# An S4 convolution with an MLP on one core: filter taps by products of two channels, a residual and some joins on TensorE, and a new order of the work

## The chip, the core and the metric

The kernel runs on one core of a Trainium2 chip. A core has five engines with their own instruction streams: TensorE (PE, matrix products; its weight loads are listed apart as PEld), VectorE (DVE), ScalarE (ACT), GpSimd (POOL) and SyncE (SP, which here issues nearly all DMAs). They meet only through semaphores. The metric is the device time of one execution in microseconds (us); a smaller one is better.

## The reference

One sequence of L = 2048 rows and D = 512 channels goes through a diagonal state space convolution and an MLP, each with a residual:

```
def _A_ref(u, A_re, A_im, B_re, B_im, C_re, C_im, log_dt, Dskip):
    logdA = dt * A                                   # dt = exp(log_dt), A complex, D x N, N = 128
    P = jnp.exp(logdA[:, :, None] * l[None, None, :])
    K = jnp.einsum("dn,dnl,dn->dl", Cc, P, dB).real  # the filter: 2048 taps for each channel
    Kf, Uf = rfft2(pad(K)), rfft2(pad(u.T))
    return irfft2(Uf * Kf)[..., :L].T + u * Dskip
def _B_ref(x, w1, b1, w2, b2):
    h = gelu(layernorm(x) @ w1 + b1)                 # 512 -> 1376
    return h @ w2 + b2                               # 1376 -> 512
x = A_u
h = x + _A_ref(layernorm(x), ...)
h2 = h + _B_ref(layernorm(h), ...)
```

## The kernel before

**Tiling.** The 2048 rows are two blocks (b = 0 and 1) of 1024; the 512 channels are four chunks (c = 0 to 3) of 128, and two chunks make a pair (q = 0: chunks 0 and 1; q = 1: chunks 2 and 3). The convolution of 2048 taps becomes three products of spectra: block 0 by the filter's first half, block 1 by the first half, and block 0 by the second half into block 1. Tiles on TensorE are up to 128 x 1024 float32 in PSUM, of which there are four slots; each matrix product is followed by an evacuation (`evac`), a cast to bfloat16 in SBUF that ScalarE (L542) or VectorE (L544) does.

**Stages, by line.**
- `chain` (L1030, L1059, L1068, L1072) and `aexps` (L801) make, for each channel and state, the powers that the taps are built from: sines on ScalarE, products on VectorE, angles on TensorE.
- Taps: `kgen` (L1101 and L1102) for chunks 0 and 1, one channel for each matmul, weights of 20 columns in four column strips of the array. `kgen4` (L1132 and L1133) for chunks 2 and 3: weights of 128 columns hold four channels, the right side too (4 x 33 columns), so the product has all 16 pairs of channels of which the four of a channel with itself are used; the evacuation takes the whole tile, and the tap store `Kg[1]` has room for it. L1115 and L1142 add the skip term to the first tap.
- `carry` (L1152, four small copies for each pair, on SyncE's queue), then `kspec` (L1167) makes the filter's first spectrum step; `kstage` writes it to DRAM (`AK_d`) and reads it back in another layout by the DMA helper L554; `fstage` (L981) finishes it. `lstage` (L1195, L1214, by way of `AL_d`) does the same for the taps of the second half.
- `xspec` (L961, L981) makes the spectra of the rows.
- `inverse` for each block and chunk, in two halves fh: products of spectra on VectorE (L1243; one for block 0, two for block 1, added by L1248). For block 1 two further VectorE operations (L1251) join real and imaginary parts before TensorE; 16 matmuls L1259 follow. For block 0 there is no join, and TensorE does 32 matmuls that add the parts in PSUM. After the evacuation a transposing DMA (`turn`, L1265) gives the layout for the tail.
- `tail(b, sb)`, for halves sb of a block: L1329 spreads the result back over the rows, and the residual x is added: in block 0's first half by TensorE (an identity product, L1324, evacuated as a cast), in the other three by VectorE (L1336). L1339 takes statistics; `stats` holds the small operations and a power on GpSimd (L926); L1352 or L1354 normalises.
- `mlp(b, sb)`: L1383, gelu on ScalarE (L1385), L1405, the last addition on VectorE (L1407), stores.

**What sets the order.** Each operation is recorded with `add(engine, cost, ...)` in the order of the code. The list `ORDER` then says in which order they are issued: its n-th entry is the number of an operation (as ~i, a negative number, where an operation that two engines could do goes to the second one). Each engine executes its own operations in that order, and SyncE issues its DMAs in that order. Costs that a recorded operation names move nothing in `ORDER`; `Sched.run` uses them to estimate where TensorE would wait for more than 0.4 us behind a certain point, and puts filler matmuls there (L1510, results unused).

Of the kernel before, what the change touches and what calls it, by code (L numbers as in the profile page):

```python
# [15 lines left out]
P = 128  # L16
# [10 lines left out]
NB = 33  # L27
# [138 lines left out]
class VS(V):  # L166
# [244 lines left out]
def kernel(ctx, tc, A_u, A_A_re, A_A_im, A_B_re, A_B_im, A_C_re, A_C_im, A_log_dt, A_Dskip,  # L411
# [85 lines left out]
    S4 = take(f16, 4, 512)  # L497
    assert pos[0] <= rest0 + 8192
    pos[0] = rest0 + 8192
    Kg = [take(bf16, NB, 2, 32), at(sc0 - 512, bf16, NB, 4, 2, 32)]  # L500
    zlo = take(bf16, NB, 2, 32).lo
    AK0 = take(bf16, 16, 2 * CW).lo
    XB = XT(ar, (E0 + 16384, BA0 + 16384))
# [613 lines left out]
    def kgen4(c, pr):  # L1117
        Ar, Br, Ai, Bi = EA2[c - 2], EB[c], IA2[c - 2], IB[c]
        kg = Kg[1]
        for j0 in range(0, 32, 6):  # L1120
            S.pr = pr + 0.01 * (j0 // 6)
            p = Ps()
            n = min(6, 32 - j0)
# [20 lines left out]
    def kgof(q, g):  # L1144
        return Kg[0].ap() if q == 0 else Kg[1].ap()[:, :, g]
# [406 lines left out]
```

## Time and profile before

| | before |
|---|---|
| time, median of 3 runs | 235.97 us (235.88 to 236.08) |
| the profiled execution, its own time | 235.89 us |
| its span in the trace | 234.0 us |
| DMA | 20.33 MB in 39246 packets |
| MLP products on TensorE, L1383 and L1405 | 40.4 and 39.6 us busy |
| casts out of PSUM on ScalarE, L542 | 75, 66.6 us busy |
| sines on ScalarE, L1068 | 36, 34.5 us busy |
| spectrum products on VectorE, L1243 | 24, 28.8 us busy |
| filler matmuls on TensorE, L1510 | 53, 14.6 us busy |

The page lists for each engine how long it was busy, in what slices of the span, and by which line, operation and tile. A row of a window gives for each engine its busy time and instructions in a stretch of the span, the mean granted clock of TensorE, the busy share of the DMA engines and GB/s. A row of the chain of waits, "A <- B", says that A began when B had ended: the total, the count and the longest. A row of the timeline is start, duration (us), engine, tile, line and, where several ran in a row, their count.

### The profile page before, as it was taken

The numbers are of one execution on the slowest core, as the hardware profiler recorded it, in microseconds if no ns is written. First come the engines' busy times: TensorE is split into PE (matmuls) and PEld (weight loads), VectorE is DVE, ScalarE is ACT, GpSimd is POOL, SyncE is SP. The second block draws the span as 40 slices with busy tenths as digits, with TensorE's granted clock in tenths as the row PEclk, the third lists the DMA queues.
The fourth block names the chain that finished last, engine by engine and source line by source line (L and its number), as shares of the span: only waits on it lengthen the run. The fifth ranks groups of instructions, "written<-read, shape, count | busy, mean of one in ns | idle before, by whom it ended". The sixth has DMA issues, their size and how long they took to land.

```text
span 234.0 us, 6711 instructions
## 1 busy us (share of the span) xinstructions
PE 200.7 (86%) x2809; PEld 106.9 (46%) x2809; DVE 170.0 (73%) x304; ACT 177.3 (76%) x217; POOL 39.8 (17%) x185
## 2 busy tenths in 40 slices
PE   4206898868888899999989988899999999999993
PEld 2102633325666685456753343344444444444552
DVE  4969989998997764798999889889934884022021
ACT  5999999999999898999989897787275106806600
POOL 7950760000055520040000110100000101000000
PEclk9999999999999999999999999999999999999998
DMA  5692220100000163875589922235632072053103
GB/s 170 165 197 55 59 36 11 37 1 3 3 6 6 30 146 68 244 202 183 112 140 198 311 96 41 49 66 104 114 66 38 0 139 66 0 111 79 34 20 72
DMA packets 39246, 20.33 MB, mean 87 GB/s; under 512 B 26738, under 2 KB 37012, under 8 KB 39216
## 3 DMA queue, kind: packets, MB, share of 16 engines
q1 hardware_dynamic: 38510, 19.28, 36.1%
q0 software_dynamic: 256, 0.30, 0.8%
q8 instruction: 22, 0.36, 0.6%
q10 hardware_dynamic: 450, 0.33, 0.5%
q14 instruction: 8, 0.07, 0.1%
HBM read 8.10 MB, written 4.49 MB: 54 GB/s over the span
## 4 chain that ended last, share of the span: by engine, by line
PE 41%; ACT 13%; DVE 7%; DMA 5%; issue 4%; POOL 3%; SPq 1%; ACTq 0%; DVEq 0%
PE ps L1405 16%; PE ps L1383 13%; ACT ar L542 9%; DMA ar<-ar 3%; PE ps L1329 2%; ACT ar L1068 2%; DMA ar<-AK_d 2%; PE ps L1259 2%; PE ps L981 2%; ACT ar L1385 2%; DVE ar L1248 2%; DVE ar L1243 1%; POOL ar L926 1%; PE ps L961 1%; POOL ar L1466 1%
## 5 line engine op out<-in xcount | busy, mean ns | idle before, releaser
L542 ACT CAST ar<-ps 128x1024 bf16<-128x1024 f32 (+3 forms) x75 | 66.6, 965 | 11.8 <-PE ps L1259 5.1
L1385 ACT ACTIVATE ar<-ps,ar 128x512 bf16<-128x512 f32 (+1 forms) x44 | 28.6, 687 | 25.0 <-PE ps L1383 24.5
L1383 PE MATMUL ps<-ar 128*128 128x512 bf16 (+1 forms) x176 | 40.4, 379 | 1.5 <-ACT ar L542 1.1
L1405 PE MATMUL ps<-ar 128*128 128x512 bf16 (+3 forms) x187 | 39.6, 367 | 0.0
L1068 ACT ACTIVATE ar<-ps 128x1024 bf16<-128x1024 int16 x36 | 34.5, 1058 | 0.5 <-PE ps L1059 0.5
L1407 DVE TENSOR_TENSOR ar<-ps,ar 128x512 bf16<-128x512 f32 (+1 forms) x17 | 10.8, 653 | 29.5 <-PE ps L1405 16.3
L1243 DVE TENSOR_TENSOR ar<-ar 128x2048 bf16<-128x2048 bf16 x24 | 28.8, 1220 | 3.8 <-PE ps L1259 3.0
L1405 PEld LDWEIGHTS <-ar 128*128 128x128 bf16 (+1 forms) x187 | 18.0, 98 | 19.9 <-issue 0.4
L1383 PEld LDWEIGHTS <-ar 128*128 128x128 bf16 (+1 forms) x176 | 17.1, 100 | 21.7 <-issue 3.0
L1059 PE MATMUL ps<-ar 128*32 128x512 f16 (+1 forms) x368 | 21.6, 331 | 5.7 <-ACT ar L1068 5.6
L544 DVE CAST ar<-ps 128x1024 bf16<-128x1024 f32 (+3 forms) x20 | 21.2, 1075 | 7.0 <-PE ps L1133 3.0
L1510 PE MATMUL ps<-ar 128*128 128x512 bf16 x53 | 14.6, 412 | 13.6 <-DMA ar<-in_A_u_dram 12.2
L1030 DVE TENSOR_TENSOR ar<-ar 128x2048 bf16<-128x2048 bf16 x21 | 24.8, 1214 | 0.8 <-ACT ar L1068 0.4
L926 POOL TENSOR_TENSOR ar<-ar 128x4 f32<-128x4 f32 (+1 forms) x6 | 9.3, 1544 | 93.9 <-DVE ar L603 42.2
L801 ACT ACTIVATE ar<-ar 128x1024 bf16<-128x1024 f32 x16 | 15.7, 1041 | 1.1 <-DVE ar L613 1.1
L1059 PEld LDWEIGHTS <-ar 128*32 128x32 f16 x368 | 9.3, 97 | 15.8 <-issue 13.5
L961 PE MATMUL ps<-ar 128*32 128x512 bf16 x256 | 15.9, 380 | 0.2 <-ACT ar L542 0.2
L1259 PE MATMUL ps<-ar 64*128 64x128 bf16 x384 | 13.6, 217 | 1.1 <-ACT ar L542 1.1
L1510 PEld LDWEIGHTS <-ar 128*128 128x128 bf16 x53 | 4.9, 102 | 21.0 <-issue 17.5
L1259 PEld LDWEIGHTS <-ar 64*128 64x128 bf16 x384 | 11.1, 94 | 6.7 <-issue 2.7
L619 DVE SCALAR_TENSOR_TENSOR ar<-ar 128x4 f32<-128x4 f32 (+5 forms) x37 | 10.2, 282 | 5.3 <-POOL ar L926 3.5
L981 PE MATMUL ps<-ar 128*32 128x512 bf16 (+1 forms) x256 | 13.0, 328 | 0.2
(118 smaller groups left out, 293.7 us busy)
## 6 DMA issues: line engine op xcount, KB each, us to landing
ar<-in_A_u_dram SPq DMA_DIRECT2D x4, 512.0 KB
AK_d<-ar SPq DMA_DIRECT2D x4, 512.0 KB
ar<-AK_d SPq DMA_DIRECT2D x4, 512.0 KB
out_dram<-ar SPq DMA_DIRECT2D x30, 64.0 KB
ar<-in_B_w_dram SPq DMA_DIRECT2D x4, 344.0 KB
ar<-ar SPq DMA_DIRECT2D x20, 64.0 KB
ar<-in_B_w_dram SPq DMA_DIRECT2D x2, 640.0 KB
AL_d<-ar POOLq DMA_DIRECT2D x8, 36.0 KB, 4.0
```

The lines of the kernel that those rows point to most:

```text
L542: act.copy(out_fn(), in_fn())
L544: dve.tensor_copy(out_fn(), in_fn())
L961: pe.matmul(pst(p)[32 * cg:32 * cg + 32, 512 * z:512 * z + 512], lhsT=BD.ap()[:, 32 * f + 2 - 2 * jl:32 * f + 34 - 2 * jl], rhs=un[2 * (2 ...
L1030: dve.tensor_tensor(o, o[:, 1].unsqueeze(1).to_broadcast([P] + list(o.shape[1:])), f[:, :, ::-1, ::-1] if rev else f, ALU.mult)
L1059: pe.matmul(pst(p)[32 * g:32 * g + 32, 256 * j:256 * (j + n)].rearrange("p (a b) -> p a b", a=n), lhsT=W2[DELTAS.index(d)].ap(), rhs=S2[g] ...
L1068: add("ACT", c_act(1024), lambda e, o_=o_, i_=i_: act.activation(o_(), i_(), ACT.Sin, scale=SINSC), r=[p, TBL], w=[sc[cs]])
L1243: dve.tensor_tensor(pieces(o).rearrange("p z (a r d) -> p a z r d", a=4, r=2), k, x, ALU.mult)
L1259: pe.matmul(pst(p)[:, 512 * h + 128 * k:512 * h + 128 * k + 128], lhsT=o[z].ap()[rows, k, r, :], rhs=TP[w].ap()[rows, f0 // 2 + k, :], sta ...
L1383: pe.matmul(pst(p)[:fs, 512 * z:512 * z + 512], lhsT=w1s[dc].ap()[:, fc * P:fc * P + fs], rhs=ybuf.ap().rearrange("p (t c) k -> p c t k", ...
L1385: add("ACT", c_act(512, 1), lambda e, p=p, z=z, fc=fc, fs=fs: act.activation(hT.ap()[:fs, fc, :], pst(p)[:fs, 512 * z:512 * z + 512], ACT. ...
L1405: pe.matmul(pst(p)[:, 512 * z + c0:512 * z + c1], lhsT=hT.ap()[:fs, fc, 128 * t:128 * t + 128], rhs=w2s[fc].ap()[:fs, c0:c1], start=(fc == ...
L1510: pe.matmul(slots[z][:, 0:512], lhsT=identb.ap(), rhs=hs[15].ap(), start=True, stop=True)
```

## The change

1. Chunks 2 and 3: `kgen4` becomes `kgen2`. A matmul multiplies two channels (64 weight columns by 2 x 33 columns), for two halves g of the array's columns, so there are 256 matmuls of half the width and height instead of 128, and six PSUM tiles to evacuate instead of twelve. `Kg[1]` halves. The additions L1142 shrink with it.
2. Chunks 0 and 1 of block 1 are no longer joined on VectorE: `mix` is true for chunks 2 and 3 alone, and TensorE does 32 matmuls for each of the four halves.
3. All of block 0's residual is now on TensorE (four identity products more), and those four tiles are evacuated by casts instead of additions.
4. The cost that the power in `stats` names goes from 0.3 to 1.5, the one of L1329 to 0.85.
5. A new list `ORDER`, for 8 joins, 6 tap tiles and their matmul groups less.

```
--- before.py
+++ after.py
-    49, 1, 0, 50, 2, 12, 15, 5, 52, 11, 13, 40, 3, 16, 88, 74, 17, 167, 4, 51, 43, 18, 19, 73, 53, 54, 56, 146, 139, 33, 55, 20, 70, 94, 68, 21, 75,
...
+    1, 49, 12, 0, 2, 138, 166, 4, 50, 15, 11, 13, 16, 52, 17, 146, 18, 51, 19, 54, 20, 73, 53, 74, 21, 3, 137, -57, 43, 22, -283, 75, 23, 55, 76, 24,
...
-    Kg = [take(bf16, NB, 2, 32), at(sc0 - 512, bf16, NB, 4, 2, 32)]
+    Kg = [take(bf16, NB, 2, 32), at(sc0, bf16, NB, 2, 2, 32)]
...
-        POOL(0.3, lambda: gp.tensor_tensor(buf[3].ap(), buf[1].ap(), mhalf.ap().to_broadcast([P, n]), ALU.pow), r=[buf[1], mhalf], w=[buf[3]], pr=pr)
+        POOL(1.5, lambda: gp.tensor_tensor(buf[3].ap(), buf[1].ap(), mhalf.ap().to_broadcast([P, n]), ALU.pow), r=[buf[1], mhalf], w=[buf[3]], pr=pr)
...
-    def kgen4(c, pr):
+    def kgen2(c, pr):
...
-        for j0 in range(0, 32, 6):
+        for j0 in range(0, 32, 12):
             p = Ps()
-            n = min(6, 32 - j0)
-            h = (n + 1) // 2
+            h = min(12, 32 - j0) // 2
             for b in range(2):
                 def fn(e, p=p, j0=j0, b=b, h=h):
                     for jj in range(h):
                         i = j0 + h * b + jj
-                        o = pst(p)[:, 512 * b + 132 * jj:512 * b + 132 * jj + 132].rearrange("p (k g) -> p k g", g=4)
-                        w = lambda v: v.ap().rearrange("p g a i -> p (g a) i")[:, :, i]
-                        x = lambda v: v.ap()[:, :, 4 * i:4 * i + 4]
-                        pe.matmul(o, lhsT=w(Ar), rhs=x(Br), start=True, stop=False)
-                        pe.matmul(o, lhsT=w(Ai), rhs=x(Bi), start=False, stop=True)
+                        for g in range(0, 4, 2):
+                            o = pst(p)[32 * g:32 * g + 64, 512 * b + 66 * jj:512 * b + 66 * jj + 66].rearrange("p (k g) -> p k g", g=2)
+                            w = lambda v: v.ap()[:, g:g + 2].rearrange("p g a i -> p (g a) i")[:, :, i]
+                            x = lambda v: v.ap()[:, :, 4 * i + g:4 * i + g + 2]
+                            pe.matmul(o, lhsT=w(Ar), rhs=x(Br), start=True, stop=False, tile_position=(0, 32 * g))
+                            pe.matmul(o, lhsT=w(Ai), rhs=x(Bi), start=False, stop=True, tile_position=(0, 32 * g))
...
-            evac(ofn, ifn, 2 * h * 4 * NB, [p], [kg])
+            evac(ofn, ifn, 2 * h * 2 * NB, [p], [kg])
...
-        return Kg[0].ap() if q == 0 else Kg[1].ap()[:, :, g]
+        return Kg[0].ap() if q == 0 else Kg[1].ap()[:, :, g & 1]
...
-            if b:
+            mix = b and c > 1
+            if mix:
                 for r, op in enumerate((ALU.subtract, ALU.add)):
...
-            terms = [(0, 0, 0), (0, 1, 2)] if b else [(0, 0, 0), (1, 1, 1), (0, 1, 2), (1, 0, 2)]
+            terms = [(0, 0, 0), (0, 1, 2)] if mix else [(0, 0, 0), (1, 1, 1), (0, 1, 2), (1, 0, 2)]
...
-                    if first:
+                    if b == 0:
                         pe.matmul(o, lhsT=identb.ap(), rhs=hs[8 * b + j].ap(), start=True, stop=False)
...
-                if not first:
+                if b:
                     add("DVE", c_dve(512, 1, True), lambda e, src=src, hh=hh: dve.tensor_tensor(hh.ap(), src(), hh.ap(), ALU.add), r=[p, hh], w=[hh], hv=0)
                 else:
                     evac(lambda hh=hh: hh.ap(), src, 512, [p], [hh])
...
-            (kgen if q == 0 else kgen4)(c, 5.1 + 4 * c)
+            (kgen if q == 0 else kgen2)(c, 5.1 + 4 * c)
```

From L182 on, where `ORDER` ends, the changed kernel's lines have numbers lower by one; behind `mix` in `inverse` they agree again.

**What the new order moves.** On VectorE, around the end of the taps of chunks 0 and 1: the products L1072 belong to the chain, the cast with 33 x 10 elements evacuates the last tap tile, and L1115 (128x32) is the skip term behind it, for which the first spectrum product waits. L619, L603 and L947 belong to the row statistics and their normalised rows. Before:

```order
L1072 TENSOR_TENSOR ar<-ar 128x16x128 x2
L1115 TENSOR_TENSOR ar<-ar 128x32
L619 SCALAR_TENSOR_TENSOR ar<-ar 128x8
L1072 TENSOR_TENSOR ar<-ar 128x16x128
L947 TENSOR_SCALAR ar<-ar 128x512
L603 TENSOR_TENSOR ar<-ar 128x8
L1072 TENSOR_TENSOR ar<-ar 128x16x128
L544 CAST ar<-ps_67 128x33x10
L1115 TENSOR_TENSOR ar<-ar 128x32
```

Of the change, at the same place (numbers lower by one; L592 and L602 are pieces of other tables, L1466 is the memset of the pads, which GpSimd did before):

```order
L1114 TENSOR_TENSOR ar<-ar 128x32
L602 TENSOR_TENSOR ar<-ar 128x512
L592 TENSOR_SCALAR ar<-ar 128x32
L1466 MEMSET ar 128x8x192
L1071 TENSOR_TENSOR ar<-ar 128x16x128
L543 CAST ar<-ps_65 128x33x10
L1114 TENSOR_TENSOR ar<-ar 128x32
L1071 TENSOR_TENSOR ar<-ar 128x16x128 x2
```

Two products and the statistics that stood ahead of the last cast and its skip term now stand behind them, and the memset has come in.

On SyncE's queue, from the carries of chunks 0 and 1 to the first transposes of block 0 (AK_d_68 belongs to pair 0, AK_d_69 to pair 1). Before:

```order
L1152 DMA ar<-ar 7x2048 x4
L554 DMA AK_d_68<-ar 128x8x256 x2
L1152 DMA ar<-ar 7x32x64 x4
L554 DMA ar<-AK_d_68 128x2048 x2
L554 DMA AK_d_69<-ar 128x8x256 x2
L554 DMA ar<-in_B_w_dram 96x512
L554 DMA ar<-AL_d_70 18x4x256 x4
L554 DMA ar<-AK_d_69 128x2048 x2
L554 DMA ar<-AL_d_71 18x4x256
L1265 DMA_TRANSPOSE ar<-ar 128x16x128 x4
```

Of the change, the same stretch up to the third load of w1 (two more reads and the first four transposes follow behind it):

```order
L1151 DMA ar<-ar 7x2048 x4
L553 DMA AK_d_68<-ar 128x8x256 x2
L553 DMA ar<-AK_d_68 128x2048 x2
L1151 DMA ar<-ar 7x32x64 x4
L553 DMA AK_d_69<-ar 128x8x256
L553 DMA ar<-in_B_w_dram 128x1376
L553 DMA AK_d_69<-ar 128x8x256
L553 DMA ar<-in_B_w_dram 128x1376
L553 DMA ar<-AL_d_70 18x4x256 x2
L553 DMA ar<-AK_d_69 128x2048
L553 DMA ar<-AL_d_70 18x4x256
L553 DMA ar<-in_B_w_dram 128x1376
```

The reads of AK_d_68 now stand ahead of the four carries of pair 1, and three loads of w1 (128x1376) have come in ahead of the transposes.

On VectorE, block 1's first chunk, second half, which runs together with block 0's tail. Before:

```order
L1243 TENSOR_TENSOR ar<-ar 128x4x2x256 x2
L1352 TENSOR_SCALAR ar<-ar 128x512
L1248 TENSOR_TENSOR ar<-ar 128x2048
L1336 TENSOR_TENSOR ar<-ps_64,ar 128x512
L1251 TENSOR_TENSOR ar<-ar 128x4x128
L1339 BN_STATS ar<-ar 128x6
L1251 TENSOR_TENSOR ar<-ar 128x4x128
L1336 TENSOR_TENSOR ar<-ps_64,ar 128x512
```

Of the change:

```order
L1242 TENSOR_TENSOR ar<-ar 128x4x2x256 x2
L1247 TENSOR_TENSOR ar<-ar 128x2048
L1339 BN_STATS ar<-ar 128x6
L1242 TENSOR_TENSOR ar<-ar 128x4x2x256 x2
L1339 BN_STATS ar<-ar 128x6
L1247 TENSOR_TENSOR ar<-ar 128x2x1024
```

The joins L1251 and the residual additions L1336 are gone from between the products and sums, and the next half's products have moved up.

More of the change, by code (lines that the diff above doesn't have):

```diff
@@ L1115, in kgen @@
         add("DVE", c_dve(32), lambda e: dve.tensor_tensor(kg.ap()[:, 0, c & 1], kg.ap()[:, 0, c & 1], Dz.ap()[:, c, :], ALU.add), r=[kg, Dz], w=[kg])
-    def kgen4(c, pr):
+    def kgen2(c, pr):
         Ar, Br, Ai, Bi = EA2[c - 2], EB[c], IA2[c - 2], IB[c]
         kg = Kg[1]
-        for j0 in range(0, 32, 6):
-            S.pr = pr + 0.01 * (j0 // 6)
+        for j0 in range(0, 32, 12):
+            S.pr = pr + 0.01 * (j0 // 12)
             p = Ps()
-            n = min(6, 32 - j0)
-            h = (n + 1) // 2
+            h = min(12, 32 - j0) // 2
             for b in range(2):
@@ L1128, in fn @@
                         i = j0 + h * b + jj
-                        o = pst(p)[:, 512 * b + 132 * jj:512 * b + 132 * jj + 132].rearrange("p (k g) -> p k g", g=4)
-                        w = lambda v: v.ap().rearrange("p g a i -> p (g a) i")[:, :, i]
-                        x = lambda v: v.ap()[:, :, 4 * i:4 * i + 4]
-                        pe.matmul(o, lhsT=w(Ar), rhs=x(Br), start=True, stop=False)
-                        pe.matmul(o, lhsT=w(Ai), rhs=x(Bi), start=False, stop=True)
-                add("PE", 0.13 * h, fn, r=[EA2, Br, IA2, Bi], w=[p], new=[p] if b == 0 else [], hv=1)
+                        for g in range(0, 4, 2):
[4 more added lines that the diff above has]
+                            pe.matmul(o, lhsT=w(Ai), rhs=x(Bi), start=False, stop=True, tile_position=(0, 32 * g))
+                add("PE", 0.14 * h, fn, r=[EA2, Br, IA2, Bi], w=[p], new=[p] if b == 0 else [])
             def ofn(j0=j0, h=h):
@@ L1139, in ifn @@
             def ifn(p=p, h=h):
-                return pst(p).rearrange("p (b q) -> p b q", b=2)[:, :, 0:132 * h].rearrange("p b (i n) -> p n b i", i=h)
-            evac(ofn, ifn, 2 * h * 4 * NB, [p], [kg])
-        add("DVE", c_dve(128), lambda e: dve.tensor_tensor(kg.ap()[:, 0, :, c & 1, :], kg.ap()[:, 0, :, c & 1, :], Dz.ap()[:, c, :].unsqueeze(1).to_broadcast([P, 4, 32]), ALU.add), r=[kg, Dz], w=[kg])
+                return pst(p).rearrange("p (b q) -> p b q", b=2)[:, :, 0:66 * h].rearrange("p b (i n) -> p n b i", i=h)
+            evac(ofn, ifn, 2 * h * 2 * NB, [p], [kg])
+        add("DVE", c_dve(64), lambda e: dve.tensor_tensor(kg.ap()[:, 0, :, c & 1, :], kg.ap()[:, 0, :, c & 1, :], Dz.ap()[:, c, :].unsqueeze(1).to_broadcast([P, 2, 32]), ALU.add), r=[kg, Dz], w=[kg])
     def kgof(q, g):
-        return Kg[0].ap() if q == 0 else Kg[1].ap()[:, :, g]
+        return Kg[0].ap() if q == 0 else Kg[1].ap()[:, :, g & 1]
     def carry(q, pr):
@@ L1259, in fn @@
                             pe.matmul(pst(p)[:, 512 * h + 128 * k:512 * h + 128 * k + 128], lhsT=o[z].ap()[rows, k, r, :], rhs=TP[w].ap()[rows, f0 // 2 + k, :], start=(n == 0), stop=(n == len(terms) - 1), tile_position=(64 * h, 0))
-            add("PE", 0.235 * len(terms), fn, r=(o[:1] if b else o) + TP, w=[p], new=[p])
+            add("PE", 0.235 * len(terms), fn, r=(o[:1] if mix else o) + TP, w=[p], new=[p])
             evac(lambda f0=f0: zw.ap()[:, :, f0:f0 + 8].rearrange("p q (k h) -> p q k h", h=2), lambda p=p: pst(p).rearrange("p (h k q) -> p q k h", h=2, k=4), 1024, [p], [zw])
@@ L1328, in fn @@
                             rhs = multi(zt[0].lo + (8 * h + j) * 256, zt[1].lo - zt[0].lo, bf16, NCH, CW)
-                            pe.matmul(o[64 * h:64 * h + 64], lhsT=DD.ap()[:, di].rearrange("p a b -> p (a b)"), rhs=rhs, start=(n == 0 and not first), stop=(n == len(terms) - 1))
-            add("PE", 0.85 if first else 0.43 * (1 + b), fn, r=[identb, DD] + [hs[8 * b + 4 * sb + 2 * jp + z] for z in range(2)] + ZT0 + (ZT1 if b else []), w=[p], new=[p])
+                            pe.matmul(o[64 * h:64 * h + 64], lhsT=DD.ap()[:, di].rearrange("p a b -> p (a b)"), rhs=rhs, start=(n == 0 and b == 1), stop=(n == len(terms) - 1))
+            add("PE", 0.85, fn, r=[identb, DD] + [hs[8 * b + 4 * sb + 2 * jp + z] for z in range(2)] + ZT0 + (ZT1 if b else []), w=[p], new=[p])
             for z in range(2):
```

63 rows, old and new, of the table ORDER are left out of this document.

## Prediction

> **What bounds the kernel now.** I read three views in this order: the page (shares of the engines and the chain of work that ended last), the windows (busy time of each engine in stretches that I chose by the chain), and the chain itself in order of time.
>
> ```profile
> PE 200.7 (86%) x2809; PEld 106.9 (46%) x2809; DVE 170.0 (73%) x304; ACT 177.3 (76%) x217; POOL 39.8 (17%) x185
> PE 41%; ACT 13%; DVE 7%; DMA 5%; issue 4%; POOL 3%; SPq 1%; ACTq 0%; DVEq 0%
> core 0: us, PE busy (x) PEld busy (x) DVE busy (x) ACT busy (x) POOL busy (x), PEclk, DMA share, GB/s
> 20.00:77.00 57.00, 47.72 (x1118) 27.22 (x1120) 53.23 (x101) 56.49 (x67) 15.18 (x17) 1.00 0.10 21
> 77.00:100.00 23.00, 22.92 (x408) 14.68 (x408) 15.31 (x29) 20.73 (x25) 4.23 (x5) 1.00 0.51 130
> 100.00:126.00 26.00, 24.59 (x613) 15.97 (x600) 23.55 (x23) 24.48 (x28) 2.40 (x4) 1.00 0.73 161
> 126.00:153.00 27.00, 24.43 (x236) 10.33 (x234) 24.11 (x42) 23.58 (x31) 2.61 (x3) 1.00 0.46 128
> 153.00:177.00 24.00, 23.67 (x172) 11.22 (x167) 18.37 (x25) 15.12 (x22) 0.00 (x0) 1.00 0.51 95
> 177.00:230.00 53.00, 53.00 (x271) 24.76 (x268) 20.04 (x44) 19.70 (x30) 2.02 (x2) 1.00 0.26 53
> 126.00:153.00 27.00, 5.43 (x22) 1.90 (x22) 1.00 0.46 128
> 76.92 1.04 PE ps L1167 x16
> 191.98 8.64 PE ps L1383 x40
> 230.07 0.42 DVE ar L1407
> ```
>
> The kernel has three parts. From 20 to 77 us ScalarE is busy 56.49 of 57.00 us and VectorE 53.23: the sines and exponentials and their products set the pace, and the change leaves their number as it is. From 77 us on TensorE is the engine to count. Its own work from the first L1167 at 76.92 to its end at 230.07 can be written as a ledger: 153.1 us, of which it is idle in the four windows from 77 to 177 for 0.08, 1.41, 2.57 and 0.33 us, together 4.4. The row with x22 is the same stretch 126 to 153 for the filler matmuls of L1510 alone: 5.4 us of the "busy" time are fillers, which stand where TensorE waits anyway. So **9.8 us of that ledger are lost**, 8.0 of them between 126 and 153. From 177 on nothing is lost. The end is therefore the start of L1167, plus the work behind it, plus what is lost. The granted clock is 1.00 in every window, so it plays no part.
>
> **The change part by part.** All sums are against the profiled execution's own 235.89 us (span 234.0, of which 230.07 is the start of the last VectorE addition; what lies behind it, an addition and two stores, stays). The median of the three runs is 235.97, 0.08 away, and I carry no correction.
>
> *A. The start of L1167.*
>
> ```profile
> PEld L1167 <- DVE ar L1115: 1.5, 1, 1.5
> DVE ar L619 <- POOL ar L926: 3.5, 4, 1.5
> 67.14 2.71 POOL ar L1466
> 69.85 3.45 POOL ar L926
> ```
>
> TensorE waited 1.5 us for L1115, the last step of the last block-0 tap tile. That step stood late on VectorE: behind a product that itself came after a wait of 1.5 us for GpSimd's power L926 (3.45 us), which had stood behind the memset L1466 (2.71 us). In the new order the cast and L1115 stand behind the first of the five products, and the memset is on VectorE. What is late next is the last chain matmul and ScalarE's last sine, so the 1.5 us go but no more. Against it stand moved pieces in the first 77 us (two 1024-element conversions and the memset go from GpSimd to VectorE, some statistics go behind the chain); VectorE has 3.8 us idle between 20 and 77 to take them. Bounds: +1.0 (they delay the chain) to -1.7; **taken -1.5**.
>
> *B. Taps of chunks 2 and 3.* Before: 128 matmuls of 128 weight columns and 132 columns. Now: 256 of 64 weight columns and 66 columns, on two column halves of the array.
>
> ```profile
> 84.00:88.00 4.00, 4.00 (x64) 4.00 (x63) 2.32 (x7) 4.00 (x6) 0.00 (x0) 1.00 0.44 109
> L1132 PE MATMUL ps<-ar 128*128 128x132 bf16 x64 | 8.7, 229 | 0.0
> 57.20:58.40 1.20, 1.20 (x86) 1.20 (x78) 1.01 (x2) 1.20 (x3) 0.00 (x0) 1.00 0.00 0
> L1101 PE MATMUL ps<-ar 128*20 128x33 bf16 x256 | 9.8, 247 | 0.0
> 120.46 1.08 PE ps L1259 x32
> 161.71 0.56 PE ps L1259 x16
> ```
>
> The window 84 to 88 holds only these matmuls: 64 touch 4.00 us, and since one lasts 229 ns, one starts every 4.23/64 = 66 ns; 128 cost 8.5 us. The new shape is in no row. The nearest from below are the taps of chunks 0 and 1, 20 weight columns in four column strips: 86 touch 1.20 us, (1.20+0.25)/86 = 17 ns each, so 256 would cost 4.3 us. From above, the same 17 ns per 20 columns scaled to 64 columns are 54 ns, 13.8 us. Between them stands L1259, which works on two halves of the array as the new taps do: 1.08/32 = 34 ns, 256 cost 8.6 us. I take that row: **0.0**, with -4.2 and +5.3 as ends.
>
> A rule of the Trainium skill speaks against this part: "TensorE: Matmul & The Clock Gate", section "LDWEIGHTS (loading the stationary operand)", gives a weight load the number of columns over 1.2 GHz, and "TensorEngine Tiling (Array Packing)", section "Restrictions", says that column tiling switches the fast weight load off. By them 64 columns would take 53 ns, the upper end above; the trace agrees for 20 columns (17 ns) and for 128 columns in one piece it can only be the fast load (66 ns, not 107). It is the rival 1 below.
>
> The evacuation halves:
>
> ```profile
> L542 ACT CAST ar<-ps 128x792 bf16<-128x792 f32 x7 | 5.5, 871 | 0.2 <-PE ps L1133 0.2
> L544 DVE CAST ar<-ps 128x792 bf16<-128x792 f32 x3 | 2.8, 974 | 1.3 <-PE ps L1133 1.3
> L544 DVE CAST ar<-ps 128x264 bf16<-128x264 f32 x2 | 1.0, 498 | 1.7 <-PE ps L1133 1.7
> ```
>
> Twelve tiles (9.3 us of the two engines) become six: by the change's order four of 792 and one of 528 on ScalarE, one of 528 on VectorE, about 3.5 + 1.2 us at these durations. 4.6 us go, but between 77 and 100 TensorE is busy 22.92 of 23.00 us, so the evacuation is cover there and its loss is worth nothing at once. It is worth something later, in E.
>
> *C. Joins of chunks 0 and 1 of block 1.* Eight VectorE additions L1251 go, and four tiles get 32 instead of 16 matmuls: by the two L1259 rows 4 x (1.08 - 0.56) = **+2.1 us** of TensorE work. Bounds: 1.9 to 2.3, all of it in the stretch where TensorE waits.
>
> *D. Residual of block 0's second half.*
>
> ```profile
> 127.80 0.55 PE ps L1329 x4
> 128.35 0.32 PE ps L1324
> ...
> 130.65 0.34 PE ps L1329 x2
> 140.01 0.33 DVE ar L1251
> 139.41 0.60 DVE ar L1336
> L542 ACT CAST ar<-ps 128x512 bf16<-128x512 f32 x5 | 2.8, 600 | 0.6 <-PE ps L1329 0.6
> ```
>
> A tile without the identity product takes 0.55 us (127.80). The two tiles of the first half, which have it, run from 128.35 to 130.99, 1.32 each. Two tiles change: 2 x (1.32 - 0.55) = **+1.5 us** on TensorE. Four additions L1336 leave VectorE, at 0.60 us of its queue each, and four casts of 0.60 us come to ScalarE.
>
> *E. What is lost between 77 and 177.* Between 126 and 153 TensorE loses 8.0 us. The chain of waits there runs over VectorE (L1243, L1248, L1251, L1336, L1339) and ScalarE's casts, so what these two have to do in that stretch sets the loss. VectorE gets rid of 8 x 0.33 + 4 x 0.60 = 5.0 us of its 24.11; that is the upper bound of what comes back. ScalarE gets up to 2.4 us more on its 23.58, which leaves 2.6 as the lower bound if it takes the lead. Neither row is nearer, so I take the middle, **-3.8**. The new order holds 6 fillers behind the first L1167, where the old one has 22 between 126 and 153; an order has no durations, so I use it for the direction alone. Outside this stretch 1.8 us are idle, most of it around 117 us:
>
> ```profile
> 89.91 3.35 SPq L1152 DMA_DIRECT2D ar<-ar  x4
> 93.38 1.01 SPq L554 DMA_DIRECT2D ar<-AK_d  x2
> 111.36 6.11 DMA ar<-ar
> ```
>
> The block-0 spectrum was read back at 93.38, behind four small copies of L1152 that waited for the taps of chunks 2 and 3 until 89.91. Now the read stands ahead of them, so block 0's inverse can come some microseconds sooner, and the transposing DMA of 6.11 us, for whose buffer ScalarE waited at 117.5, starts sooner as well. Half of the 1.8: **-0.9**, bounds 0 to -1.8. What is queued behind on the same queue: three weight loads of 344 KB now go ahead of these transposes (rival 2).
>
> **Sum:** -1.5 + 0.0 + 2.1 + 1.5 - 3.8 - 0.9 = -2.6 us, **233.3 us**.
>
> **The rivals.**
>
> 1. *The finer tap products cost TensorE more than they save* (ends slower). Place: 78 to 88 us, where TensorE has no idle time. Price: 54 ns for each of 256, +5.3 us. With the rest of the sum -2.6 + 5.3 = +2.7, 238.6 us. It decides from 34 + 2600/256 = 44 ns per matmul upwards. For it: 17 ns at 20 columns fits a load paid by the column. Against it: L1259 brings 128 weight columns for 64 rows every 34 ns.
>
> 2. *A new wait takes the place of the lost time* (also slower). The three weight loads, 1.03 MB, at the 161 GB/s of the window 100 to 126 are 6.4 us of transfer ahead of the transposes, which block 0's tail waits for. If that keeps the lost 9.8 us as they are, C and D come on top: -1.5 + 3.6 = +2.1, 238.0 us. Against it: those transposes themselves have more lead than before, and the loads gone ahead are missing behind them, where the DMA share is high now.
>
> 3. *It cancels.* TensorE's added 3.6 us fit into time that it waited anyway, the earlier start is eaten by moved work in the first part, and VectorE's chain of products for block 1 ends when it did: about 235.9. For it: that chain keeps its two products and one sum for each half of a chunk.
>
> 4. *More comes back.* Taps at 17 to 25 ns (-2 to -4.2) or the whole 5.0 us in E with the whole 1.8: 229 to 231.
>
> That the change doesn't do what it says can be excluded: the order shows the new shapes, the eight missing additions and the four added identity products.
>
> **How the numbers follow.** The forecast gets 0.55 (its own range 231.3 to 235.3), rival 4 gets 0.15, rival 3 0.10, rival 1 0.11, rival 2 0.09. A change of 0.2%, 0.5 us, is about what a measurement of this kernel can tell from none. Faster: 0.55 + 0.15 and a little of rival 3, 0.72. Within 0.2%: 0.10. Slower: 0.18. The range of 229.5 to 237.5 us holds the forecast, rival 3 and most of rival 4, and leaves out rivals 1 and 2 (0.20).
>
> **What would show it.** A: the first L1166 of the new profile starts between 75 and 76. B: the taps L1131/L1132 start every 34 ns; 50 or more is rival 1, below 25 rival 4. C and D: 32 inverse matmuls in 1.1 us in the first two chunks of block 1, tiles with the identity at 1.3. E: idle time plus fillers behind the first L1166 are 5 us, not 9.8; and TensorE runs without a gap for the last 55 us or more. The forecast is wrong if the start of L1166 is later than 77, if the lost time is still 9 us, or if some engine other than TensorE ends the last 50 us.

## The result and the profile after

The changed kernel takes 244.78 us (median of 4 runs, 244.25 to 245.74), the one before 235.94 (235.88 to 236.08, 4 runs): a ratio of 1.038, 95% interval 1.034 to 1.042. It is 8.8 us slower; 233.3 were forecast, and 237.5 was the upper end. The profiled execution took 245.16 us with a span of 243.4, so 9.3 us more than the one of before.

The page of the changed kernel (busy time, the chain that ended last) and its windows, in the same stretches as before; behind "PEclk" stands the mean granted clock:

```profile
PE 211.5 (87%) x2998; PEld 115.9 (48%) x2998; DVE 171.5 (70%) x302; ACT 171.1 (70%) x209; POOL 34.9 (14%) x181
PE 56%; DVE 5%; ACT 4%; issue 2%; DMA 1%; SPq 1%; DVEq 0%
PEclk9999999999999955999999999979999999999998
core 0: us, PE busy (x) PEld busy (x) DVE busy (x) ACT busy (x) POOL busy (x), PEclk, DMA share, GB/s
77.00:100.00 23.00, 22.34 (x372) 17.69 (x368) 10.89 (x27) 11.85 (x14) 4.36 (x5) 0.70 0.38 107
100.00:126.00 26.00, 24.02 (x576) 14.71 (x564) 21.40 (x21) 22.54 (x25) 2.41 (x4) 1.00 0.74 176
126.00:153.00 27.00, 25.88 (x370) 12.29 (x364) 24.74 (x38) 26.02 (x34) 1.03 (x1) 1.00 0.46 112
153.00:177.00 24.00, 21.84 (x207) 10.70 (x207) 20.21 (x27) 14.38 (x20) 1.01 (x1) 0.93 0.53 90
```

TensorE is on more of the chain (56% instead of 41%), and the clock, 1.00 in all of these windows before, is 0.70 in the window of the taps and 0.93 in the one from 153. Its own timeline at the start of the ledger, and the windows around the two places:

```profile
74.26 1.39 PE L1058 MATMUL ps<-ar 128*32 128x256 f16 x32
75.58 1.04 PE L1166 MATMUL ps<-ar 20*128 20x512 bf16 x16
78.37 1.04 PE L1166 MATMUL ps<-ar 27*128 27x512 bf16 x16 [0.66 <-DMA ar<-ar]
79.35 0.33 PE L1131 MATMUL ps<-ar 128*64 128x66 bf16 x2
...
L1131 PE MATMUL ps<-ar 128*64 128x66 bf16 x128 | 14.9, 301 | 0.0
80.00:84.00 4.00, 4.00 (x76) 4.00 (x76) 3.02 (x8) 3.97 (x5) 0.00 (x0) 1.00 0.47 126
88.00:92.00 4.00, 4.00 (x70) 4.00 (x70) 1.36 (x5) 0.80 (x1) 3.20 (x4) 0.50 0.75 266
94.40:97.00 2.60, 2.60 (x28) 0.69 (x29) 1.49 (x5) 0.60 (x1) 0.00 (x0) 0.50 0.04 10
155.40:158.60 3.20, 1.04 (x21) 0.39 (x20) 1.23 (x1) 2.45 (x4) 0.00 (x1) 1.00 0.02 5
158.60:162.60 4.00, 4.00 (x39) 2.07 (x40) 3.87 (x5) 1.70 (x2) 1.01 (x1) 0.58 0.10 19
```

The first spectrum product starts at 75.58 (76.92 before). One tap product lasts 0.30 us and several overlap, so their price is the time from start to start: one starts every (4.00 + 0.30)/76 = 57 ns at full clock; the 256 fill 79.35 to 94.36, 15.0 us where 8.7 us of tap products stood. The clock falls to half in the midst of them, although TensorE is busy in 4.00 of 4.00 us, and what follows runs at half clock until 97.7: 3.3 us, of which half is lost. Later TensorE stands still for 2.2 us at 156 and is then at 0.58 for 4 us.

The ledger of the prediction, for the changed kernel: start -1.34; taps +6.3; half clock behind them +1.6; added matmuls of C and D +3.3; idle time (0.66 + 1.98 + 1.12 + 2.16 in the four windows) and 1.8 of fillers, together 7.7 instead of 9.8, -2.1; half clock from 158.6 on 4 x 0.42 = +1.7. Sum +9.5, measured in the trace +9.3.

### The profile page after: what moved, and what is told of

The parts are those of the page before. It is cut to its first block, busy times and chain, and to the rows that moved or that the text cites. A ratio compares the mean times of both kernels' runs of the same rounds, so it can differ in the third digit from the quotient of the medians.

```text
span 243.4 us, 7055 instructions
## 1 busy us (share of the span) xinstructions
PE 211.5 (87%) x2998; PEld 115.9 (48%) x2998; DVE 171.5 (70%) x302; ACT 171.1 (70%) x209; POOL 34.9 (14%) x181
## 4 chain that ended last, share of the span: by engine, by line
PE 56%; DVE 5%; ACT 4%; issue 2%; DMA 1%; SPq 1%; DVEq 0%
PE ps L1383 16%; PE ps L1405 16%; PE ps L960 6%; PE ps L1259 5%; ACT ar L541 4%; PE ps L1131 3%; PE ps L1132 3%; DVE ar L543 3%; PE ps L1329 2%; PE ps L980 2%; PE ps L1166 1%; DMA ar<-ar 1%; SPq L1151 1%; PE ps L1324 1%; DVE ar L1466 1%
## 5 line engine op out<-in xcount | busy, mean ns | idle before, releaser
L541 ACT CAST ar<-ps 128x1024 bf16<-128x1024 f32 (+4 forms) x73 | 64.8, 948 | 21.5 <-PE ps L1132 7.7
L1383 PE MATMUL ps<-ar 128*128 128x512 bf16 (+1 forms) x176 | 41.8, 388 | 0.1
L543 DVE CAST ar<-ps 128x1024 bf16<-128x1024 f32 (+4 forms) x20 | 21.9, 1109 | 7.8 <-PE ps L1132 2.5
L1058 PE MATMUL ps<-ar 128*32 128x512 f16 (+1 forms) x368 | 21.5, 331 | 4.7 <-ACT ar L1067 4.3
L1510 PE MATMUL ps<-ar 128*128 128x512 bf16 x46 | 13.3, 424 | 10.2 <-DMA ar<-in_A_u_dram 9.9
L925 POOL TENSOR_TENSOR ar<-ar 128x4 f32<-128x4 f32 (+1 forms) x6 | 7.4, 1233 | 94.6 <-DVE ar L602 64.4
L1259 PE MATMUL ps<-ar 64*128 64x128 bf16 x448 | 16.0, 219 | 4.0 <-DVE ar L1247 2.2
L1259 PEld LDWEIGHTS <-ar 64*128 64x128 bf16 x448 | 12.9, 95 | 9.8 <-issue 4.6
L960 PE MATMUL ps<-ar 128*32 128x512 bf16 x256 | 17.1, 404 | 0.1
L1058 PEld LDWEIGHTS <-ar 128*32 128x32 f16 x368 | 9.2, 97 | 14.8 <-issue 12.4
L1131 PE MATMUL ps<-ar 128*64 128x66 bf16 x128 | 14.9, 301 | 0.0
L1132 PE MATMUL ps<-ar 128*64 128x66 bf16 x128 | 14.9, 301 | 0.0
L1131 PEld LDWEIGHTS <-ar 128*64 128x64 bf16 x128 | 14.2, 210 | 0.4 <-issue 0.4
```

The costliest lines, as they stand in the source:

```text
L541: act.copy(out_fn(), in_fn())
L543: dve.tensor_copy(out_fn(), in_fn())
L960: pe.matmul(pst(p)[32 * cg:32 * cg + 32, 512 * z:512 * z + 512], lhsT=BD.ap()[:, 32 * f + 2 - 2 * jl:32 * f + 34 - 2 * jl], rhs=un[2 * (2 ...
L1058: pe.matmul(pst(p)[32 * g:32 * g + 32, 256 * j:256 * (j + n)].rearrange("p (a b) -> p a b", a=n), lhsT=W2[DELTAS.index(d)].ap(), rhs=S2[g] ...
L1131: pe.matmul(o, lhsT=w(Ar), rhs=x(Br), start=True, stop=False, tile_position=(0, 32 * g))
L1259: pe.matmul(pst(p)[:, 512 * h + 128 * k:512 * h + 128 * k + 128], lhsT=o[z].ap()[rows, k, r, :], rhs=TP[w].ap()[rows, f0 // 2 + k, :], sta ...
```

## The experiments

The runs of the kernel before lay between 235.1 and 239.2 us in the later sets, more scattered than at first, so a difference below 1 us between sets is not read; each ratio is against the runs of before in its own set.

### What the tap products cost

**Four channels again, in the new order** (the old `kgen4`, with its twelve casts put by me between those that the new list has there):

```
-            (kgen if q == 0 else kgen2)(c, 5.1 + 4 * c)
+            (kgen if q == 0 else kgen4)(c, 5.1 + 4 * c)
...
```

> The changed kernel with the taps of chunks 2 and 3 as before (products of four channels, 128 matmuls, twelve tiles), in the new order: part B of the change undone, the rest kept. Theory 1 (the finer tap products are paid by their weight columns, 256 x 58 ns = 15.0 us, and lower the clock behind them): the taps go back to about 8.7 us (-6.3) and the granted clock stays at 1.00 from 77 to 100 us (-1.7), so about 236.7 us. Theory 2 (the new order, with its weight loads ahead of the transposes, costs the time, and the taps only fill a wait): 242 us or more.

Measured 240.76 us, ratio 1.019 (1.015 to 1.024): 4 us come back, not 8. The taps are at 8.7 us and the clock stays at 1.00 until 153, as theory 1 has it; but my order of casts made the next stage wait (3.5 us of fillers from 89 to 93), and the stall at 156 with its half clock was still there. So neither number fits, and two more causes had to be parted from the taps.

**One channel at a time**, as chunks 0 and 1 have it:

```
-                        for g in range(0, 4, 2):
+                        for g in range(4):
...
+                            o = pst(p)[32 * g:32 * g + NA, 512 * b + 33 * jj:512 * b + 33 * jj + 33]
...
```

> The changed kernel with the taps of chunks 2 and 3 made one channel at a time: 512 matmuls of 20 weight columns by 33 columns in four column strips, order unchanged. Theory 1 (a column of weights costs 0.85 ns whatever the matmul): 17 ns each, 8.7 us, no lowered clock, about 236.5 us. Rival (each matmul on a part of the columns has a price of its own, which 256 showed as 58 ns and which four strips share): 512 cost as much as the 256 or more, 15 us, 244 us or more.

Measured 245.46 us, ratio 1.040 (1.036 to 1.045). Windows of it that hold only tap products:

```profile
80.00:82.00 2.00, 2.00 (x80) 2.00 (x73) 2.00 (x2) 2.00 (x1) 1.35 (x1) 1.00 0.10 17
88.00:90.00 2.00, 2.00 (x91) 1.96 (x84) 1.11 (x4) 0.49 (x1) 0.00 (x0) 0.50 0.74 208
90.00:92.00 2.00, 2.00 (x94) 2.00 (x84) 0.45 (x2) 0.07 (x1) 1.46 (x1) 1.00 0.06 16
```

A miss for theory 1 in its plain form. One product lasts 0.30 us, so at full clock one starts every (2.00 + 0.30)/94 = 24 ns from 90 to 92 and every 29 from 80 to 82; over all 512 it is 28 (they fill 79.3 to 95.5, of which TensorE waits 1.8). That is not the 17 of chunks 0 and 1 with the same shape. The rival's 15 us and 244 us came out; whether its fixed price for each product is the reason, the narrow run below decides. The clock fell here too, but at 83 us, when TensorE had just stood idle for 0.6 us, so this run does not show what lowered it. Why the same shape costs more on the tables of chunks 2 and 3 was not found out.

**Twice the moving columns**, and **half the weight columns**:

```
-                            x = lambda v: v.ap()[:, :, 4 * i + g:4 * i + g + 2]
+                            x = lambda v: v.ap()[:, :, 4 * i + g:4 * i + g + 2].unsqueeze(1).to_broadcast([P, 2, NB, 2])
...
```

> The changed kernel with 132 moving columns in each tap product instead of 66 (the 66 needed ones twice; the second copy is overwritten by the next product). Theory A (the clock is lowered because the array streams for only half of the time that a load takes): the clock stays at 1.00 in 77 to 100 us, the products still start every 55 to 60 ns, and the time falls by about 1.7 to 242 to 243 us. Theory B (the clock is lowered by the many loads, or by something else that runs at that time): it is lowered as before, and the time is 245 us or more, since 132 columns at half clock take 110 ns.

```
-                            w = lambda v: v.ap()[:, g:g + 2].rearrange("p g a i -> p (g a) i")[:, :, i]
+                            w = lambda v: v.ap()[:, g, :, i]
...
```

> The changed kernel with 32 weight columns instead of 64 in each tap product (the taps of every second channel of chunks 2 and 3 are left out), the moving 66 columns and the number of matmuls unchanged. Theory 1 (paid by the weight column): one starts every 27 to 30 ns, 7 to 8 us in all, about 236 to 238 us. Rival (a fixed price for each matmul on a half of the array's columns): 55 to 60 ns as before, 244 to 245 us.

The window from 82 to 88 us, which holds only tap products, of the wide run and of the narrow one:

```profile
82.00:88.00 6.00, 6.00 (x82) 6.00 (x80) 1.29 (x7) 2.23 (x3) 0.00 (x0) 1.00 0.65 183
...
82.00:88.00 6.00, 6.00 (x158) 6.00 (x156) 2.75 (x12) 3.66 (x5) 1.51 (x1) 1.00 0.65 182
```

Wide: 77 ns each, 20 us for all, 248.36 us in time (ratio 1.055, 1.048 to 1.061). Narrow: 40 ns, 10.2 us, 239.26 us in its one run. Neither theory had the price, and a fixed price for each product is out too: with the weights unchanged, 66 more moving columns cost 20 ns; with the data unchanged, 32 fewer weight columns save 17. **Load and stream are paid one after the other in these three shapes**: about 0.53 ns for a weight column and 0.33 for a moving one, fitted to them, give 56, 78 and 39 ns. If the load were hidden under the other half's product, one of the two changes would have cost nothing. The two prices do not carry over to other splits: for 20 by 33 columns they give 21.5 ns, where chunks 0 and 1 take 17 and the run above 28; for 128 by 132 in the whole array they give 111, where the kernel before takes 66.

On the clock theory A was right: it stayed at 1.00 during the taps with 132 columns in 77 ns and with 66 in 40 (1.7 moving columns for each ns in both), and fell with 66 in 57 (1.2). The narrow run has more loads in each microsecond and did not fall, so it is the few columns that stream, not the number of loads, that go with the fall.

Of the two rules weighed in the prediction, that of the Trainium skill's "TensorE: Matmul & The Clock Gate", section "LDWEIGHTS (loading the stationary operand)", comes near for the shape at hand (53 ns of load by it, 57 measured), but the narrow and the wide run show that the load alone is not the price: by it the wide product would still take 53 ns and the narrow one 27, and 77 and 40 were measured (53 and 27 are estimates by that section's figure). The same page, section "The mechanism", says that a weight load overlaps a running product only where the two use different groups of rows. The trace fits: L1259, split by rows, takes 34 ns with 128 weight columns, the taps, split by columns, 57 with 64. The two also differ in their number of rows and in how their operands lie in memory, and no run changed the split alone; but the whole array with weights taken from memory with the same step as the taps' has twice the columns and takes 66 ns, so that step by itself does not make 57.

**Part B alone, in the old order**, and with it the size of B:

```
-            (kgen if q == 0 else kgen4)(c, 5.1 + 4 * c)
+            (kgen if q == 0 else kgen2)(c, 5.1 + 4 * c)
...
```

> The kernel before with part B alone: the finer tap products, in the old order (a tile's matmuls and evacuation where two old tiles' stood). Theory 1 (the taps cost TensorE 15.0 us instead of 8.7 wherever they stand): 236 + 6.3 = 242.3 us, and 244 if the granted clock falls here too. Rival (only the new order makes them dear): 238 us or less.

Measured 245.86 us (244.03 to 246.02), ratio 1.036 (1.029 to 1.043). Its windows:

```profile
77.00:100.00 23.00, 23.00 (x375) 17.72 (x379) 5.27 (x18) 12.49 (x16) 4.37 (x5) 0.70 0.27 62
100.00:126.00 26.00, 25.88 (x616) 15.57 (x616) 22.58 (x23) 24.02 (x28) 2.40 (x4) 1.00 0.66 170
```

The same 0.70. From the start of L1167 at 77.00 to the last addition at 238.35 its ledger is 161.35 us instead of 153.15: **+8.2 us from the taps alone**, more than expected without the clock and as expected with it: 6.3 for the products, 0.85 for a spectrum step that then takes 1.89 us at half clock instead of 1.04, and 1.4 for three fillers behind the taps, also at half clock, less small differences. Theory 1 holds. The tap products need nothing of the rest to make the kernel as slow as the whole change makes it.

### The stall at 156 us

The timeline of VectorE in the changed kernel, then of the run in which far sums are made as two additions; L1247 adds the two products of block 1's chunk 1, second half, and L1253 is that sum in that run's file:

```profile
155.21 0.15 DVE L618 SCALAR_TENSOR_TENSOR ar<-ar 128x4 f32<-128x4 f32 x1
157.29 1.23 DVE L1247 TENSOR_TENSOR ar<-ar 128x2048 bf16<-128x2048 bf16 x1 [1.93 <-ACT ar L541]
...
154.98 0.15 DVE L618 SCALAR_TENSOR_TENSOR ar<-ar 128x4 f32<-128x4 f32 x1
155.10 1.29 DVE L1253 TENSOR_TENSOR ar<-ar 128x1024 bf16<-128x1024 bf16 x2
```

Both products were done at 155.3, yet the sum waited until a cast of ScalarE (156.25 + 1.01 = 157.26) had ended that belongs to another tile. The second product lies in two pieces far apart, written as one operand with a long stride; by the kernel's addresses the cast writes between them. In the changed line, `near` is true where the two pieces lie at most 4096 bytes apart.

```
-dve.tensor_tensor(pieces(o), pieces(o), pieces(o1), ALU.add)
+dve.tensor_tensor(pieces(o), pieces(o), pieces(o1), ALU.add) if near(o, o1) else [dve.tensor_tensor(one_piece(o, z), one_piece(o, z), one_piece(o1, z), ALU.add) for z in range(2)]
...
```

> The changed kernel with the sums of two products that lie far apart in memory made as two additions of 1024 elements instead of one of 2 x 1024 over a long stride. Theory (the sum of chunk 1's second half waited 1.9 us at 155.4 us for a cast whose tile lies between the two pieces, which it doesn't read): it starts 1.9 us sooner, TensorE's gap of 2.2 us at 156.5 us and the half clock behind it (2 us) go, and the time falls by 3 to 4 us to about 241. Rival (the sum needs that cast, or the gap has another cause): 244.5 to 245.5 us.

Measured 241.42 us, ratio 1.019 (1.011 to 1.027): 3.4 us less than the changed kernel. The sum starts at 155.10 and the gap is gone, with the half clock behind it:

```profile
155.40:158.60 3.20, 3.10 (x56) 1.90 (x55) 3.07 (x4) 3.20 (x6) 1.01 (x1) 1.00 0.02 5
158.60:162.60 4.00, 4.00 (x36) 1.77 (x35) 4.00 (x8) 3.12 (x5) 0.00 (x0) 1.00 0.80 146
```

The theory holds: the wait was for data that the sum doesn't read. In the old order the same sum exists, and that cast (found by its place, the seventh of the eight behind L1214) had ended at 147.47 + 1.02 = 148.49, ahead of the sum at 154.68; the new order put the cast's product behind MLP work and so behind the sum.

### What C, D and the order are worth

**C and D alone, in the old order**, together and apart:

```
-            terms = [(0, 0, 0), (0, 1, 2)] if b else [(0, 0, 0), (1, 1, 1), (0, 1, 2), (1, 0, 2)]
+            terms = [(0, 0, 0), (0, 1, 2)] if mix else [(0, 0, 0), (1, 1, 1), (0, 1, 2), (1, 0, 2)]
...
-                    if first:
+                    if b == 0:
                         pe.matmul(o, lhsT=identb.ap(), rhs=hs[8 * b + j].ap(), start=True, stop=False)
...
```

> The kernel before with parts C and D alone: the joins of chunks 0 and 1 of block 1 and the residual of block 0's second half on TensorE, in the old order. By step E of the prediction VectorE's 5.0 us pay for TensorE's 3.3: between 234.5 and 236.5 us. Rival (what TensorE loses there does not hang on VectorE's load): 236 + 3.3 = 239.3 us.

> The kernel before with part C alone: the joins of chunks 0 and 1 of block 1 on TensorE, in the old order. Theory S (what TensorE loses between 126 and 153 us is set by ScalarE's casts, of which C takes and adds none): the 1.8 us of matmuls fill time in which TensorE waits anyway, 235.5 to 236.7 us. Rival (TensorE's work is paid in full wherever it stands): 237.8 us or more.

> The kernel before with part D alone: the residual of block 0's second half on TensorE, in the old order. Theory S: four casts of 0.6 us go to ScalarE, which sets the loss, so the time grows by 1.5 to 2.5 us, to 237.5 to 238.5. By step E of the prediction (VectorE sets it, and is relieved of 2.4 us): 235.0 to 236.5 us.

Together 240.57 us, ratio 1.016 (1.009 to 1.022); C alone 236.75, 1.003 (1.000 to 1.006); D alone 237.26, 1.005 (1.003 to 1.007). Nothing is won in the old order. Together they cost TensorE's 3.3 us and a little, although VectorE is relieved as step E had it (windows of the run with both, and TensorE's waits from 126 to 153 in it and in the kernel before):

```profile
100.00:126.00 26.00, 23.86 (x602) 15.68 (x597) 22.78 (x22) 23.68 (x27) 2.40 (x4) 1.00 0.70 157
126.00:153.00 27.00, 24.75 (x283) 11.43 (x276) 18.85 (x30) 23.75 (x32) 1.55 (x2) 1.00 0.50 135
200.00:230.00 30.00, 29.06 (x141) 13.81 (x140) 3.58 (x6) 13.33 (x20) 0.00 (x0) 1.00 0.22 44
126.00:153.00 27.00, 4.19 (x17) 1.42 (x17) 1.00 0.50 135
...
PE ps L1260 <- ACT ar L542: 1.0, 2, 0.6
PE ps L1214 <- ACT ar L542: 0.7, 1, 0.7
PE ps L1384 <- ACT ar L542: 0.5, 1, 0.5
...
PE ps L1383 <- ACT ar L542: 1.1, 2, 0.6
PE ps L1510 <- ACT ar L542: 0.9, 1, 0.9
PE ps L1214 <- ACT ar L542: 0.5, 1, 0.5
```

The last of the windows is that of the fillers. VectorE falls from 24.11 to 18.85 us of 27, and idle time and fillers there from 8.0 to 2.25 + 4.19 = 6.4; but TensorE is idle for 2.14 us from 100 to 126 (1.41 before) and for 0.94 from 200 to 230 (none before), so nearly all of it is lost elsewhere. The waits that are named all end with ScalarE's casts, 2.2 us here and 2.5 in the kernel before. C alone, which leaves ScalarE its load, was nearly free, as theory S had it; D alone cost 1.1 us where that theory expected 1.5 to 2.5 and step E a gain. That the two together cost more than their sum is not explained.

**In the new order with four channels**, the casts better placed; then with the split sums; then without C and D:

> The run with products of four channels in the new order, mended where my own order of its casts delayed what follows: the rows for the block-0 spectrum are normalised between the casts instead of behind them, and the last tap cast stands ahead of the next stage. Theory 1 (the taps alone cost 6.3 + 1.7 us): the 3.5 us of fillers at 89 to 93 us go, 237.3 us. Rival (the rest of the new order costs as much as before): 240 us or more.

> The new order with the products of four channels (casts placed as in the last such run) and with the far sums in two instructions: both stalls of the changed kernel taken out, its joins and residual on TensorE kept. If the effects add: 239.05 less 3.4, about 235.7 us. If the stall behind the sum only hid another wait: 237.5 to 239 us.

> The same with the joins and the residual of block 0's second half back on VectorE (parts B, C and D of the change undone, its order kept, the far sums in two instructions). If C and D cost TensorE 3.3 us and give nothing back in this order either: 232.0 to 233.0 us. If this order needs VectorE relieved: as the run with both on TensorE, or slower.

Measured 239.05 us, ratio 1.008 (1.004 to 1.013); 236.39, 1.001 (0.997 to 1.005); 242.56, 1.026 (1.021 to 1.030). The first is between its two expectations. The second shows the stall's worth again, 2.7 us where 3.4 were expected, and stands level with the kernel before. The third fell to the other side: with the joins and the residual back on VectorE this order is 6 us slower. What is a loss in the old order is needed in the new one. Each list of the two was made for its own kernel, though, and the operations put back stand where I placed them; an order made afresh for each case was not tried, so these differences hold for these orders.

**The rest of the gap.** In the second of these runs TensorE was still idle for 2.0 us between 77 and 100, 1.3 of it in waits for casts, in an order that was mine. Three runs mended the casts (block 1's statistics and the table load behind the tap casts), the last two of them with C or D undone; a fourth moved two casts of the row spectrum ahead as well.

> The new order with products of four channels and the far sums in two instructions, with my casts of the taps freed: block 1's statistics and the table load stand behind the casts, and a group of the row spectrum stands ahead of the first spectrum step of pair 1. If the rest of the change (A, C, D and the order) is worth what it frees once both stalls are gone: 1.0 to 1.7 us of TensorE's 2.5 lost between 77 and 97 us come back, 234.7 to 235.4 us, faster than the kernel before. If not: 236.4 us as before this edit.

> The same with part C undone (the joins of chunks 0 and 1 of block 1 back on VectorE). If it is VectorE's chain of products that the new order needs relieved: eight additions of 0.33 us stand in that chain, 2.7 us, less 1.8 on TensorE: slower by 1 to 3 us. If C gives nothing back: faster by 1.8 us.

> The same with part D undone (the residual of block 0's second half back on VectorE). If this order needs the residual off VectorE: slower by 2 to 4 us (with C together 6 were seen). If D gives nothing back: faster by 1.5 us.

> The last mended run with two casts of the row spectrum moved ahead of block 1's statistics and rows on VectorE, for which TensorE waited 1.6 us at 94.6 us. If what was left of the gap to the kernel before is TensorE's wait between 77 and 98 us (2.9 us there, of which these casts end 2.0): 234.6 to 235.3 us, faster than the kernel before by 0.3 to 0.8%. If that wait only moves: 236.5 us.

The first is 236.60 us, ratio 1.000 (0.998 to 1.002), no faster than the run before it: the wait had only moved, to a cast of the row spectrum. C undone costs 2.2 us (238.81, 1.011, 1.006 to 1.017), D undone 2.3 (238.94, 1.010, 1.005 to 1.016): both pay in this order. The fourth is **235.13 us, ratio 0.994 (0.991 to 0.997), faster than both kernels**. Its windows:

```profile
77.00:100.00 23.00, 21.98 (x363) 14.36 (x354) 20.25 (x38) 17.94 (x20) 4.35 (x5) 1.00 0.53 146
100.00:126.00 26.00, 24.80 (x608) 15.65 (x600) 22.70 (x23) 23.89 (x27) 2.40 (x4) 1.00 0.83 176
126.00:153.00 27.00, 25.87 (x319) 12.37 (x316) 24.93 (x42) 25.55 (x35) 2.04 (x2) 1.00 0.27 78
153.00:177.00 24.00, 23.66 (x173) 10.85 (x173) 16.64 (x26) 14.79 (x21) 0.00 (x0) 1.00 0.70 124
...
77.00:100.00 23.00, 1.43 (x5) 0.40 (x5) 1.00 0.53 146
126.00:153.00 27.00, 1.21 (x4) 0.31 (x4) 1.00 0.27 78
153.00:177.00 24.00, 0.59 (x2) 0.20 (x2) 1.00 0.70 124
```

The last three rows are its fillers. From 100 to 177 us it loses 1.20 + 1.13 + 0.34 idle and 1.80 of fillers, 4.5 us; the kernel before loses 4.3 + 5.4 = 9.7 there. The new order with C and D does bring back about 5 us there, against the 3.3 that they cost. Part of it is lost again elsewhere: from 77 to 100 TensorE is idle for 1.02 us and has 1.43 of fillers, where the kernel before loses 0.08.

## Why the prediction was wrong, by its steps

**A, the start: right.** -1.5 taken, -1.34 measured. What is late next is what was named: the chain's matmuls L1058 run until L1166 starts, without a gap. What was not named is that TensorE then waits 0.66 us at 78.4 for the small copies (`DMA ar<-ar`), so half of it is given back at once.

**B, the taps: this is the step that failed.** "I take that row: 0.0" took the price of L1259, 34 ns, for the new shape. It cost 57 ns. L1259 splits the array by rows and the taps by columns, and the prediction passed over that as "two halves of the array". Rival 1 had the mechanism, the place and a price of 54 ns with a chance of 0.11, and argued against it with the same row. Its mechanism was only half of it, since the stream is paid as well as the load, and its price was short: 5.3 us became 8.2 in the run with B alone, 6.3 of taps and the rest work that ran at half clock behind them. The clock the prediction had set aside with "the granted clock is 1.00 in every window, so it plays no part". That was read from the kernel before, whose tap products stream 132 columns in 66 ns; what the new ones would stream was not asked. The prediction also says that for 128 columns in one piece "it can only be the fast load (66 ns, not 107)". The runs don't show that: at the 0.53 ns fitted above, an estimate, 128 weight columns take 68 ns without any faster load, if the stream is hidden there. No run tells the two apart.

**C and D: right in size.** +2.1 and +1.5 were forecast for TensorE; the four tiles that got 32 matmuls take 1.02 or 1.03 us (one, at half clock, 1.33), and the tiles with the identity 1.32, as taken.

**E, what comes back: less than forecast, and not for the reason given.** -3.8 and -0.9 were forecast for 77 to 177 us. In the changed kernel idle time and fillers fell by 2.1 only, and a second half clock took 1.7 of it away: the stall behind the far sum. The 0.9 around 117 us did not come: from 100 to 126 TensorE is idle for 1.98 us instead of 1.41, and behind the longer taps the transposes start at 116.17 instead of 111.36. In the fourth mended run 5.2 us are back between 100 and 177, but with what it loses from 77 to 100 only 2.9 in the whole stretch (6.9 lost instead of 9.8). The reason was VectorE's load. Relieving VectorE by itself gives nothing (the old order with C and D), and the waits of TensorE that the kernel before names between 126 and 153 all end with casts of ScalarE, of which D adds four. It was the order together with the relief that brought time back. Rival 2, the weight loads ahead of the transposes, is not seen: the one wait for a DMA that TensorE has between 77 and 180 us in the changed kernel is the 0.66 us for the small copies. For 1.5 us of waits at 116 and 122 the profile names nothing.

So in this order the finer taps cost about 6.3 us (241.42 with them, 235.13 in the fourth mended run, whose casts I also placed anew) and the stall 3.4, and they turn what is worth about -1.2 us without them into +8.8. That B costs less here than its 8.2 in the old order may be due to the six casts that it saves; this was not tried by itself.

## What to carry to other kernels

For a small matmul, read the price of a new shape from a row that splits the array the same way, and where there is none, try the shape by itself first: with two column halves weights and data both counted here. Before a product is made finer, ask what share of the time the array will stream: here the clock fell with 1.2 columns for each ns, though TensorE never waited. And an operand that reaches over far memory with one stride can wait for whatever is written between its pieces; a new order brings such a wait out.

## What the runs showed of the hardware that was not expected

The granted clock fell to 0.50 with TensorE busy without a gap: after 5 us of products of 66 columns every 57 ns, and it stayed there for 13 us. With 40 or 77 ns for 66 or 132 columns it did not fall while they ran (the narrow run's fell later, at 119 us, after 1.9 us of idle time). The Trainium skill's "TensorE: Matmul & The Clock Gate", section "What's actually happening", tells of a clock at half rate after an idle window of about 3.4 us. The second fall came behind a stall of 2.2 us, shorter than that, and went with it in the run with the split sums. The first fall shows that back-to-back products that stream little bring it about as well. In the run with one channel at a time the clock was back at 1.00 at 90 us, while the same products went on; what brings it back was not tried.

At half clock the tap products cost 61 ns instead of 57 ((4.00 + 0.30)/70), so most of their price doesn't follow the array's clock.
